# Feed-forward weights by float32 load and on-chip cast, RMS gain folded in, and a new order of all steps (linear attention, then SwiGLU)

## The chip, the cores and the metric

The kernel runs on one core of one Trainium2 chip. The metric is the device time of one execution in microseconds; the time before is the median of three runs. The profile is one further execution, recorded instruction by instruction. Engine names are those of the profile: PE (TensorE matmuls), PEld (its weight loads), DVE (VectorE), ACT (ScalarE), POOL (GpSimd), SP (SyncE, which issues most DMAs here).

## The reference

Two layers, one after the other, all in float32 at the boundary. B = 4 sequences, H = 8 heads, S = 768 steps, D = 48 per head; so 3072 tokens of H·D = 384.

```python
# linear attention with a decaying state, per (batch, head):
for t in range(S):
    y[t]  = r[t] @ (state + (u * k[t]) v[t]^T)
    state = w[t][:, None] * state + k[t] v[t]^T
# feed-forward on x = y, tokens x 384
rms = sqrt(mean(x * x, axis=-1) + 1e-6)
xn  = x / rms * rms_g
out = (silu(xn @ w_gate) * (xn @ w_val)) @ w_out     # 384 -> 1536 -> 384
```

## The kernel before

The sequence is cut into six blocks n = 0..5 of 128 steps; j = 0..3 is the batch. One attention step works on (n, j): 128 steps, 8 heads. One feed-forward step works on a block n: all four batches, so 512 tokens, and one of 12 groups f of 128 hidden units.

Every piece of work is a named step `name.n.j` (or `name.n.f`), and the string `ORDER` lists all of them. The kernel issues them in that order, and each engine and each DMA queue does its own part of them strictly in that order; semaphores are set where data or a buffer is needed. So the order is written out by hand, and an engine that waits holds up all that stands behind it in its own queue.

The steps of attention for one (n, j): `load_r`, `load_k`, `load_v`, `load_w` (SP, 192 KB each; in blocks 0 and 1 one `load_w` of 384 KB serves both); `ln` (ACT, logarithm of the decay); `cs_mm` (PE, running sums by a mask matmul), `cs_add` (DVE); `exp_r`, `exp_k` (ACT); `r_mul`, `k_mul` (DVE; `k_mul` on POOL from block 1); `rk_pe` (PE transposes) with `rk_tr` (ACT copy) in blocks 0 and 1, `rk_tr` alone (a transposing DMA from SP) later; `q_mm` (PE), `q_mask_e`, `q_copy_o`, `q_mask_o` (masks); `st_mm`, `st_new` (state); `bonus_mul`, `bonus_v` (POOL), `bonus_sum` (DVE); `cast_v` (ACT in blocks 0 and 1, POOL later); `y_mm` (PE), `x_add` (DVE).

Between the layers: `x_sq` (ACT, sum of squares), `x_rstd` (ACT in block 0, two POOL instructions later), `xn_mul` (ACT). Then x has to be transposed: in blocks 0 to 3 by `xn_pe` (three PE transposes) and `xn_out` (DVE, which also multiplies by rms_g); in blocks 4 and 5 by `xn_tr` (a transposing DMA from SP) and `xn_gain` (POOL, the multiplication by rms_g).

The feed-forward steps for a block: `gate_mm`, `val_mm` (three matmuls of 128x512 each), `silu` (ACT), `h_mul` (DVE), `o_mm` (12 matmuls of 128x384), `o_out` (copy), `out_dma`. `gate_mm` alternates between two PSUM banks (ring a), `val_mm` between two others (ring b); the rest uses four (ring q). ACT uses two function tables, one for exp and ln, one for silu, and reloads at each change.

The weights come by DMAs of POOL's software queue that cast from float32 to bfloat16 on the way: `load_gv.g.h` brings gate (h = 0) and value weights (h = 1) in two groups (`GV = (0, 4, 12)`: hidden groups 0 to 3, then 4 to 11), `load_wo.g` the output weights in three groups. `warm` steps are matmuls of zeros that compute nothing; there are 48 of them, all before or just at the start of the feed-forward of block 0.

Of the kernel before, what the change touches and what calls it, by code (L numbers as in the profile page):

```python
# [30 lines left out]
rk_pe.0.1 warm.15.0 warm.14.0 load_k.0.3 bonus_mul.0.3 load_r.1.1 load_r.1.0 load_k.1.1 load_v.1.1 load_r.1.2 ln.0.3
load_k.1.3 warm.20.0 warm.37.0 warm.2.0 warm.22.0 warm.23.0 warm.5.0 warm.3.0 rk_pe.0.0 warm.24.0 load_gv.0.1
load_k.1.2 load_v.1.0 load_w.2.1 warm.25.0 load_v.1.2 load_w.2.0 load_v.1.3 load_r.2.1 load_r.2.0 load_w.2.2 warm.32.0
warm.27.0 st_mm.0.0 st_new.0.0 load_w.2.3 cs_mm.0.2 rk_tr.0.1 q_mm.0.1 warm.19.0 rk_tr.0.0 exp_r.0.2 cast_v.0.1
r_mul.0.2 warm.7.0 cs_mm.0.3 q_mask_e.0.1 q_mm.0.0 warm.6.0 warm.18.0 warm.11.0 warm.26.0 warm.1.0 warm.21.0 warm.36.0
exp_k.0.2 w_tot.0.2 k_mul.0.2 rk_pe.0.2 q_mask_e.0.0 bonus_sum.0.2 bonus_v.0.2 exp_r.0.3 w_tot.0.3 q_mask_o.0.0
r_mul.0.3 warm.39.0 y_mm.0.0 warm.9.0 cs_mm.1.0 cast_v.0.3 q_mask_o.0.1 x_add.0.0 load_k.2.1 load_gv.0.0 cast_v.0.2
exp_k.0.3 k_mul.0.3 rk_tr.0.2 q_mm.0.2 q_mask_o.0.2 q_mask_e.0.2 y_mm.0.1 x_add.0.1 exp_r.1.0 bonus_sum.0.3 r_mul.1.0
rk_pe.0.3 cs_mm.1.1 x_sq.0.0 warm.34.0 x_rstd.0.0 rk_tr.0.3 q_mm.0.3 q_mask_o.0.3 exp_r.1.1 exp_k.1.0 exp_k.1.1
warm.40.0 warm.35.0 x_sq.0.1 x_rstd.0.1 xn_mul.0.0 xn_mul.0.1 y_mm.0.2 q_mask_e.0.3 warm.44.0 warm.42.0 x_add.0.2  # L40
warm.41.0 st_mm.0.3 st_new.0.3 warm.43.0 x_sq.0.2 x_rstd.0.2 w_tot.1.1 w_tot.1.0 bonus_v.0.3 y_mm.0.3 x_add.0.3
x_sq.0.3 xn_mul.0.2 x_rstd.0.3 xn_pe.0.0 xn_out.0.0 st_mm.0.2 xn_pe.0.1 cs_mm.1.3 exp_r.1.3 st_new.0.2 xn_out.0.1
r_mul.1.1 load_gv.1.0 k_mul.1.0 st_mm.0.1 warm.47.0 rk_pe.1.0 warm.45.0 st_new.0.1 xn_pe.0.2 xn_out.0.2 cs_mm.1.2
xn_mul.0.3 exp_k.1.3 xn_pe.0.3 r_mul.1.3 xn_out.0.3 cast_v.1.1 k_mul.1.1 load_gv.1.1 rk_pe.1.1 st_mm.1.1 exp_k.1.2
exp_r.1.2 w_tot.1.2 r_mul.1.2 w_tot.1.3 bonus_mul.1.3 val_mm.0.2 val_mm.0.3 warm.46.0 gate_mm.0.2 gate_mm.0.3 rk_tr.1.1
# [637 lines left out]
```

## Time and profile before

| | |
|---|---|
| median of the runs | 203.19 us (203.01, 203.19, 203.19) |
| span of the profiled execution, first to last instruction | 202.2 us |
| busy: PE, DVE, ACT, POOL | 192.6, 146.1, 136.6, 134.3 us |
| granted TensorE clock, mean | 0.999 |
| DMA moved | 32.41 MB, of it 28.58 MB on the hardware queue and 3.54 MB on the software queue |

The profiled execution is told by its span alone; the timed runs are 0.8 to 1.0 us longer than that span, and 1.0 us is taken here for what lies around it (203.19 less 202.2). In the lists below the two numbers in front of a row are the start and the duration in microseconds. "busy" of PE contains the modelled end of each matmul, so what a matmul costs is read from the distance between the starts of two that follow each other.

### The profile page before, as it was taken

To read this page: it belongs to the slowest core of one execution; us is meant where nothing else is said; L and a number is where in the kernel's file an instruction comes from. 1 tells how busy PE (TensorE), PEld (TensorE's weight loads), DVE (VectorE), ACT (ScalarE), POOL (GpSimd) and SP (SyncE) were. 2 spreads that over 40 slices of the span, in tenths; PEclk is the share of its full clock that TensorE was granted. 3 is DMA by queue.
4 is the path that set the end of the run, shared out by engine and by line. 5 is a ranking of instruction groups with operands and counts; after the bars stand their busy time and mean duration, and the time that the engine had idled before them with its cause. 6 is when DMAs were issued, how large, how long until landed. Compare 5 with 4: busy or idle time off the path is not lost.

```text
span 202.2 us, 4444 instructions
## 1 busy us (share of the span) xinstructions
PE 192.6 (95%) x1600; PEld 113.5 (56%) x1600; DVE 146.1 (72%) x289; ACT 136.6 (68%) x278; POOL 134.3 (66%) x198
## 2 busy tenths in 40 slices
PE   1999988899999999999999999999999999999994
PEld 1564655455666555665556665555555555555562
DVE  6257796658999699987988889788878972146521
ACT  2577699688998557997566978679867764046300
POOL 6527599658789966899789898859898742400000
PEclk9999999999999999999999999999999999999999
DMA  6999999989999999958999978996184022103022
GB/s 152 243 244 177 209 182 202 202 161 201 199 192 221 196 179 238 225 133 194 177 231 245 206 171 195 216 241 134 24 192 112 15 68 71 45 3 117 0 97 99
DMA packets 121566, 32.41 MB, mean 160 GB/s; under 512 B 116420, under 2 KB 120392, under 8 KB 121544
## 3 DMA queue, kind: packets, MB, share of 16 engines
q1 hardware_dynamic: 119504, 28.58, 67.2%
q0 software_dynamic: 2032, 3.54, 9.7%
q8 instruction: 12, 0.20, 0.4%
q14 instruction: 10, 0.08, 0.1%
q10 hardware_dynamic: 8, 0.00, 0.0%
HBM read 25.96 MB, written 4.72 MB: 152 GB/s over the span
## 4 chain that ended last, share of the span: by engine, by line
PE 79%; SPq 8%; DMA 8%; POOL 2%; issue 1%; ACT 0%; POOLq 0%
PE ps_av L598 12%; PE ps_bu L598 12%; PE ps_bv L598 10%; PE ps_au L598 10%; PE ps_qx L630 8%; PE ps_qv L630 7%; SPq L244 7%; DMA wg_sb<-in_moe_w_gate_dram 6%; PE ps_qz L630 5%; PE ps_qu L630 3%; SPq L257 2%; DMA kt<-in_k_dram 2%; PE ps_qu L487 1%; PE ps_av L406 1%; PE ps_qu L515 1%
## 5 line engine op out<-in xcount | busy, mean ns | idle before, releaser
L630 PEld LDWEIGHTS <-ht 128*128 128x128 bf16 x300 | 28.3, 98 | 16.9
L231 ACT ACTIVATE sg<-ps_av 128x512 bf16<-128x512 f32 x38 | 22.7, 598 | 18.4 <-PE ps_av L598 16.8
L616 DVE TENSOR_TENSOR ht<-ps_bu,sg 128x512 bf16<-128x512 f32 x38 | 26.1, 686 | 11.7 <-PE ps_bu L598 8.4
L598 PEld LDWEIGHTS <-wg_sb 128*128 128x128 bf16 x216 | 22.8, 114 | 20.2 <-DMA wg_sb<-in_moe_w_gate_dram 2.1
L598 PEld LDWEIGHTS <-wv_sb 128*128 128x128 bf16 x216 | 23.2, 114 | 19.3 <-DVE xnt L580 0.2
L616 DVE TENSOR_TENSOR ht<-ps_bv,sg 128x512 bf16<-128x512 f32 x34 | 23.3, 686 | 12.2 <-PE ps_bv L598 8.8
L452 POOL TENSOR_TENSOR ruk<-rt,kt 128x384 f32<-128x384 f32 x24 | 24.0, 1000 | 11.1 <-DMA kt<-in_k_dram 6.0
L598 PE MATMUL ps_av<-xnt,wg_sb 128*128 128x512 bf16 x114 | 30.9, 380 | 0.4 <-DMA wg_sb<-in_moe_w_gate_dram 0.4
L231 ACT ACTIVATE sg<-ps_au 128x512 bf16<-128x512 f32 x34 | 20.4, 599 | 16.0 <-PE ps_au L598 14.6
L598 PE MATMUL ps_bu<-xnt,wv_sb 128*128 128x512 bf16 x114 | 30.9, 380 | 0.0
L598 PE MATMUL ps_au<-xnt,wg_sb 128*128 128x512 bf16 x102 | 27.7, 381 | 0.8 <-DMA wg_sb<-in_moe_w_gate_dram 0.8
L598 PE MATMUL ps_bv<-xnt,wv_sb 128*128 128x512 bf16 x102 | 27.7, 380 | 0.0
L453 POOL TENSOR_TENSOR ruk<-ruk,u_bc 128x384 f32<-128x384 f32 x24 | 23.9, 997 | 1.9
L462 POOL TENSOR_TENSOR ydiag<-vt,diag 128x384 f32<-128x384 f32 x24 | 19.7, 830 | 0.9 <-DVE diag L457 0.8
L446 POOL TENSOR_TENSOR rk<-kt,ek 128x384 bf16<-128x384 f32 x20 | 19.9, 1003 | 0.3 <-ACT ek L231 0.3
L505 POOL TENSOR_SCALAR_AFFINE_SELECT qts<-qts 128x512 bf16<-128x512 bf16 x20 | 12.5, 636 | 10.7 <-ACT qts L498 10.7
L630 PE MATMUL ps_qx<-wo_sb,ht 128*128 128x384 bf16 x96 | 16.9, 326 | 0.0
L630 PE MATMUL ps_qv<-wo_sb,ht 128*128 128x384 bf16 (+1 forms) x96 | 15.9, 316 | 0.0
L558 ACT ACTIVATE xn<-xb,rstd 128x384 bf16<-128x384 f32 x24 | 14.1, 608 | 1.2 <-POOL rstd L554 1.2
L457 DVE TENSOR_REDUCE diag<-ruk 128x8 f32<-128x384 f32 x24 | 12.9, 543 | 2.7 <-POOL ruk L453 2.7
L231 ACT ACTIVATE lw<-wt 128x384 bf16<-128x384 f32 (+1 forms) x20 | 11.2, 579 | 4.6 <-DMA wt<-in_w_dram 4.5
L229 ACT ACT_TABLE_LOAD x10 | 12.8, 1283 | 1.8 <-PEq L667 1.6
(153 smaller groups left out, 368.2 us busy)
## 6 DMA issues: line engine op xcount, KB each, us to landing
rt<-in_r_dram SPq DMA_DIRECT2D x24, 192.0 KB, 3.9
kt<-in_k_dram SPq DMA_DIRECT2D x24, 192.0 KB, 3.9
vt<-in_v_dram SPq DMA_DIRECT2D x24, 192.0 KB, 3.7
out_dram<-ob SPq DMA_DIRECT2D x23, 192.0 KB, 2.1
wt<-in_w_dram SPq DMA_DIRECT2D x16, 192.0 KB, 3.9
wt<-in_w_dram SPq DMA_DIRECT2D x4, 384.0 KB, 4.6
wo_sb<-in_moe_w_out_dram POOLq DMA_DIRECT2D x3, 384.0 KB, 5.2
wg_sb<-in_moe_w_gate_dram POOLq DMA_DIRECT2D x1, 768.0 KB, 12.0
```

What stands on the lines that cost most here:

```text
L229: nc.scalar.preload_act_table_set(table_name)
L231: return nc.scalar.activation(**kw).ins
L244: dmas["load_" + which, n, j] = nc.sync.dma_start(out=inp[which, n, j], in_=t[j, :, n * L:(n + 1) * L, :].rearrange("h t d -> t h d")).ins
L446: eng.tensor_tensor(out=rk[:, n % 2, j, 1, :, 0:D], in0=inp["k", n, j], in1=bank["cs_k", n, j][:, 0:DM].rearrange("p (h d) -> p h d", h=H) ...
L452: nc.gpsimd.tensor_tensor(out=ruk[n, j], in0=inp["r", n, j], in1=inp["k", n, j], op=ALU.mult)
L453: nc.gpsimd.tensor_tensor(out=ruk[n, j], in0=ruk[n, j], in1=u_bc, op=ALU.mult)
L457: nc.vector.tensor_reduce(out=diag[n, j].rearrange("p h o -> p (h o)"), in_=ruk[n, j], axis=mybir.AxisListType.X, op=ALU.add)
L462: nc.gpsimd.tensor_tensor(out=ydiag[n, j], in0=inp["v", n, j], in1=diag[n, j].to_broadcast([128, H, D]), op=ALU.mult)
L558: nc.scalar.activation(out=xn, in_=xb[n, j], func=AF.Copy, scale=rstd[n, j][:, 1:2])
L598: nc.tensor.matmul(ps, lhsT=units(ws, c, f), rhs=xnt[n][:, c, :], start=(c == 0), stop=(c == KC - 1))
L616: nc.vector.tensor_tensor(out=ht[n][:, f, :], in0=bank.pop(("v", n, f)), in1=bank.pop(("sg", n, f)), op=ALU.mult)
L630: nc.tensor.matmul(ps[:, cols], lhsT=ht[n][:, f, b * L:(b + 1) * L], rhs=wo_sb[:, f, cols], start=(f == 0), stop=(f == FC - 1))
```

## The change

The weights are loaded as float32 by SP's hardware queue into staging buffers, nine loads of 768 KB: gate and value weights in three groups each (12 hidden units in groups of 4), output weights in three. There are four staging buffers: two of their own, and two that lie in one of the two buffers of `ht` (the hidden activations), which is free until block 1. New steps cast from there to bfloat16: `cast_gv.g.0` on ACT and `cast_gv.g.1` on DVE, three instructions of 128x512 each, multiplying by the column of rms_g that belongs to the partition; `cast_wo.g` on ACT, one instruction of 128x1536. With rms_g in the weights, `xn_out` becomes a plain copy and `xn_gain` is gone. `x_sq` scales by the root of 1/384 and has a 385th column that contributes eps, so `x_rstd` on POOL is one instruction instead of two. x lives in one buffer per batch (`xbuf`) instead of four rotating ones. Some rings are one smaller (`ydiag` 6 to 5, `rkT` 6 to 5, `ek` 4 to 3, `vb` 9 to 8).

The order of all steps is another one. In it blocks 2 and 3 transpose x by `xn_tr` too, so `xn_pe` and `xn_out` remain for blocks 0 and 1. There are 34 `warm` steps instead of 48, and some of them use the banks of rings a and b. ACT changes its function table four more times.

```diff
-    GV = (0, 4, 12)
     FG = 4
...
+    stage_own = persist.tile([128, 2, FG * DM], FP32)
+    stage_ht = pt.tile([128, 2, FG * DM], FP32, name="ht", bufs=NHT)
+    def stage(i):
+        return (stage_own, stage_own, stage_ht, stage_ht)[i % 4][:, i % 2]
     def load_gv(g, h):
...
-        i = nc.gpsimd.dma_start(out=dst[g], in_=s[:, cols].rearrange("(c p) f -> p c f", p=128)).ins
...
+        nc.sync.dma_start(out=stage(2 * g + h).rearrange("p (c f) -> p c f", c=KC),
+                          in_=(moe_w_gate, moe_w_val)[h][:, g * FG * 128:(g + 1) * FG * 128].rearrange(
+                              "(c p) f -> p c f", p=128))
+    def cast_gv(g, h):
+        s = stage(2 * g + h).rearrange("p (c f) -> p c f", c=KC)
+        for c in range(KC):
+            if (g, h) in GAIN_ACT:                      # gate weights
+                nc.scalar.activation(out=(wg_sb, wv_sb)[h][g][:, c, :], in_=s[:, c, :], func=AF.Copy, scale=gT[:, c:c + 1])
+            else:
+                nc.vector.tensor_scalar(out=(wg_sb, wv_sb)[h][g][:, c, :], in0=s[:, c, :], scalar1=gT[:, c:c + 1],
+                                        scalar2=None, op0=ALU.mult)
     def load_wo(g, _):
-        i = nc.gpsimd.dma_start(out=wo_sb[...], in_=moe_w_out[...]).ins
+        nc.sync.dma_start(out=stage(6 + g).rearrange("p (c m) -> p c m", c=FG), in_=moe_w_out[...])
+    def cast_wo(g, _):
+        dst, s = wo_sb[:, g * FG:(g + 1) * FG, :].rearrange("p c m -> p (c m)"), stage(6 + g)
+        nc.scalar.copy(out=dst, in_=s)                  # g in WO_ACT = (0, 1, 2)
...
     def x_sq(n, j):
-        nc.scalar.activation(out=junk, in_=xb[n, j], func=AF.Square, accum_out=rstd[n, j][:, 0:1])
+        nc.scalar.activation(out=junk, in_=xbuf[:, j], func=AF.Square, scale=DM ** -0.5,
+                             accum_out=rstd[n, j][:, 0:1])
...
     def x_rstd(n, j):                                   # blocks 1 to 5
-            nc.gpsimd.tensor_scalar(out=ss, in0=ss, scalar1=1.0 / DM, scalar2=eps, op0=ALU.mult, op1=ALU.add)
             nc.gpsimd.tensor_tensor(out=rstd[n, j][:, 1:2], in0=ss, in1=mhalf, op=ALU.pow)
...
     def xn_out(n, j):
-            nc.vector.tensor_tensor(out=xnt[n][:, :, j * L:(j + 1) * L], in0=ps,
-                                    in1=gT.to_broadcast([128, KC, L]), op=ALU.mult)
-    def xn_gain(n, c):
...
+        nc.vector.tensor_copy(out=xnt[n][:, :, j * L:(j + 1) * L], in_=ps)
```

The new order from the first weight load to the first output matmul of block 0, cut to the steps that the prediction speaks of (the rest of the list is as long again for each block):

```
... load_v.0.2 ... load_k.1.0 ... load_r.1.2 load_r.1.0 load_gv.0.0 ... load_gv.0.1 ... load_k.1.2 ... load_gv.1.0
... load_k.1.3 ... load_v.1.1 ... load_gv.1.1 ... xn_out.0.1 xn_mul.0.2 k_mul.1.2 cast_gv.0.0 xn_pe.0.2 ...
xn_out.0.2 cast_gv.0.1 gate_mm.0.3 exp_k.1.3 ... gate_mm.0.2 val_mm.0.2 ... silu.0.3 ... load_gv.2.0 ...
cast_gv.1.0 ... gate_mm.0.4 ... cast_gv.1.1 ... cast_gv.2.0 ... load_gv.2.1 ... load_wo.1.0 ... gate_mm.0.9 ...
load_wo.0.0 ... cast_gv.2.1 ... load_wo.2.0 ... cast_wo.1.0 ... cast_wo.0.0 ... cast_wo.2.0 ... o_mm.0.0 o_mm.0.2
```

More of the change, by code (lines that the diff above doesn't have):

```diff
@@ L31 @@
[L31 to L45, printed above, removed]
@@ new lines @@
+x_add.0.3 x_sq.0.3 q_mask_e.0.2 st_mm.0.3 warm.20.0 r_mul.1.3 ln.2.0 q_mask_o.0.2 bonus_v.0.2 cast_v.0.2 x_rstd.0.3
+w_tot.1.3 load_gv.1.0 st_new.0.0 rk_pe.1.1 warm.21.1 rk_tr.1.1 load_k.1.3 xn_mul.0.3 y_mm.0.2 warm.22.0 warm.23.1
+warm.24.1 warm.25.2 bonus_mul.1.1 x_add.0.2 q_mm.1.1 k_mul.1.0 x_sq.0.2 st_new.0.3 bonus_mul.1.0 st_mm.0.2
+q_copy_o.1.1 r_mul.1.0 w_tot.1.0 xn_pe.0.0 load_v.1.1 xn_out.0.0 cs_mm.1.2 x_rstd.0.2 xn_pe.0.3 bonus_sum.1.1
+q_mask_o.1.1 exp_r.1.2 xn_out.0.3 load_gv.1.1 rk_pe.1.0 exp_k.1.2 xn_pe.0.1 warm.26.1 warm.27.1 r_mul.1.2 w_tot.1.2
@@ L351, in load_wo @@
[L351 to L360 removed]
+    wg_sb = [persist.tile([128, KC, FG * 128], BF16, name="wg_sb%d" % g) for g in range(FC // FG)]
```

257 lines of the change are left out of this document (120 added, 137 removed).

## The prediction

> **What bounds the kernel now.** I read the busy shares by slice first, then the chain that ended last in order of time. On the page, one digit is the busy share of a fortieth of the span:
>
> ```profile
> span 202.2 us, 4444 instructions
> PE   1999988899999999999999999999999999999994
> ```
>
> The chain (start, duration, what):
>
> ```profile
> 18.64 3.76 DMA kt<-in_k_dram
> 22.47 1.00 POOL ruk L452
> ...
> 27.90 11.95 DMA wg_sb<-in_moe_w_gate_dram
> 39.90 0.84 PE ps_av L598 x3
> 40.74 0.65 PE ps_au L598 x3
> ...
> 198.30 1.00 PE ps_qu L630 x12
> 199.32 0.32 ACT ob L639
> ```
>
> Two parts. Up to 39.90 the chain is input loads on SP, then POOL, which issues a weight load late because it stands behind POOL's arithmetic, then that load. From 39.90 to 199.3 it is PE alone, one matmul behind another, three matmuls of 128x512 in 0.65 us. There no other engine's speed matters. So the change is worth three things: how much useful PE work is done by what time in the head, PE work taken away, and new gaps.
>
> **The head, by PE work.** Costs of steps are distances between starts, from the timeline of PE:
>
> ```profile
> 28.08 0.36 PE L535 MATMUL ps_qu<-vb,qts 128*128 128x48 bf16 x8
> 28.28 0.34 PE L569 MATMUL ps_qv<-ident,xn 128*128 128x128 bf16 x3
> 28.73 0.33 PE L515 MATMUL ps_qx<-vb,rk 128*128 128x96 bf16 x4
> 28.89 0.33 PE L569 MATMUL ps_qz<-ident,xn 128*128 128x128 bf16 x3
> 29.06 0.49 PE L391 MATMUL ps_av<-lw,mw 128*128 128x384 bf16 x2
> ```
>
> The first of these is a y_mm of block 0, 0.20 (28.08 to 28.28), the third a st_mm, 0.16, the fourth an xn_pe, 0.17. Both orders have the whole PE part of block 0 and the same steps of block 1 done when the dense part begins (eight cs_mm, six rk_pe, five q_mm, four y_mm, four xn_pe), with two differences: before 39.90 the old kernel has also done seven gate and value steps (7 x 0.65 = 4.55) and one st_mm (0.16), 4.7 us together. So a new dense part that starts with its first gate step at X corresponds to X + 4.7 against 39.90.
>
> X needs two things: the first gate weights cast, and x of block 0 through ACT (in the new order cast_gv.0.0 stands right behind xn_mul.0.2).
>
> *Transfers.* SP's issues:
>
> ```profile
> 0.80 0.45 SPq L244 DMA_DIRECT2D rt<-in_r_dram  x1
> ...
> 25.64 1.30 SPq L244 DMA_DIRECT2D vt<-in_v_dram  x1
> ```
>
> Between the two lie 25 issues, four of 384 KB and 21 of 192 KB: 5568 KB in 24.84 us, 224 KB per us. In the new order four of 384 and 19 of 192 stand ahead of load_gv.0.0: 5184 KB, so it is issued at 0.8 + 23.1 = 23.9. A weight chunk's own time comes from the two large loads, issue rows and times to landing:
>
> ```profile
> 27.90 0.80 POOL L346 DMA_DIRECT2D wg_sb<-in_moe_w_gate_dram  x1
> 30.63 0.80 POOL L346 DMA_DIRECT2D wv_sb<-in_moe_w_val_dram  x1
> kt<-in_k_dram SPq DMA_DIRECT2D x24, 192.0 KB, 3.9
> wg_sb<-in_moe_w_gate_dram POOLq DMA_DIRECT2D x1, 768.0 KB, 12.0
> wv_sb<-in_moe_w_val_dram POOLq DMA_DIRECT2D x1, 768.0 KB, 13.5
> ```
>
> They land at 39.9 and 44.1: 4.2 us for what is two new chunks (768 KB in bfloat16, 1536 KB read), so 2.1 each; at SP's 224 KB per us it would be 3.4, the other end. With 2.1, load_gv.0.0 lands at 23.9 + 3.9 + (2.1 - 0.9) = 29.0, load_gv.0.1 at 31.1, the other chunks with the inputs between them at 34, 38, 40, 44.7, 46.8, 48.9 and 51.0.
>
> *ACT.* From its first logarithm at 5.09 to its first silu table load at 34.65:
>
> ```profile
> 5.09:34.65 29.56, 28.23 (x298) 16.81 (x296) 20.08 (x46) 22.68 (x50) 19.39 (x22) 1.00 1.07 210
> ACT lw L231 <- DMA wt<-in_w_dram: 4.5, 2, 2.3
> ```
>
> The fourth pair of the first row is ACT: 22.68 busy, 6.9 idle. The new list up to cast_gv.0.0 has the same steps but for one exp_k and one cast_v less and one ln and one q_copy_o more: 22.8. Of the idle time 4.5 was two waits for load_w; the new order issues two of these first of all, so I take these waits as gone and keep 2.4 (ends: 0 and 6.9). The first load_w is issued one issue earlier, so ACT starts at 4.6: 4.6 + 22.8 + 2.4 = 29.8, after the landing at 29.0. Then the cast:
>
> ```profile
> L231 ACT ACTIVATE sg<-ps_av 128x512 bf16<-128x512 f32 x38 | 22.7, 598 | 18.4 <-PE ps_av L598 16.8 <-DVE ht L616 1.0
> L558 ACT ACTIVATE xn<-xb,rstd 128x384 bf16<-128x384 f32 x24 | 14.1, 608 | 1.2 <-POOL rstd L554 1.2
> L374 ACT CAST vb<-vt 128x384 bf16<-128x384 f32 x8 | 4.0, 504 | 0.7 <-DMA vt<-in_v_dram 0.7
> 32.05 0.47 ACT L231 ACTIVATE ek<-ps_bu 128x384 f32<-128x384 f32 x1
> 32.42 0.50 ACT L374 CAST vb<-vt 128x384 bf16<-128x384 f32 x1
> ```
>
> 128 more elements cost 0.094 us (598 against 504), a scale by partition 0.104 (608 against 504), and the next one starts 0.1 before the last ends (32.05 + 0.47 against 32.42). So one instruction of cast_gv is 0.504 + 0.094 + 0.104 - 0.1 = 0.60, a cast_gv 1.8. X = 31.6; 31.6 + 4.7 = 36.3; the dense part comes 3.6 earlier.
>
> **PE work taken away.** Blocks 2 and 3 lose eight xn_pe of 0.17: 1.35 us off the dense part.
>
> **New gaps.** First, o_mm.0.0 needs cast_wo.2.0 for its ninth matmul. From cast_gv.0.0 to the end of cast_wo.2.0 ACT has: three cast_gv 5.4; three cast_wo of 1536 elements, 0.504 + 9 x 0.094 - 0.1 = 1.25 each, 3.75; twelve silu 6.0; one table load; three rk_tr, three q_copy_o, four cast_v, two x_sq, an xn_mul and an exp:
>
> ```profile
> L229 ACT ACT_TABLE_LOAD x10 | 12.8, 1283 | 1.8 <-PEq L667 1.6
> L478 ACT COPY rkT<-ps_qz 128x1024 bf16<-128x1024 bf16 x3 | 3.0, 1007 | 1.4 <-PE ps_qz L469 1.4
> L498 ACT CAST qts<-ps_qv 128x512 bf16<-128x512 f32 x5 | 2.9, 581 | 1.1 <-PE ps_qv L489 1.1
> ```
>
> 1.3 + 3 x 0.9 + 3 x 0.48 + 4 x 0.4 + 2 x 0.6 + 0.5 + 0.4 = 9.1; together 24.3. So 29.8 + 24.3 = 54.1 without an idle moment, while PE, with 24 gate and value steps (15.6) and fourteen short attention steps (4.2, by such distances) between X and o_mm.0.0 and eight matmuls of 0.16 in it, is there at 31.6 + 21.1 = 52.7: a gap of 1.4. The last chunk (51.0) is not what is late. The Trainium skill, ScalarE: Activation LUTs, section What ACT_TABLE_LOAD costs, gives an instruction 186 ns and 0.833 ns per element: that agrees with 504 for 384, and would make a cast_wo 0.12 dearer and the total 0.35 us later.
>
> Second, the transposes of block 2. Behind y_mm.2.2 ACT has a table load, eight further steps of 0.4 to 0.6 and waits for POOL, xn_mul.2.2 ends about 6.1 behind it; the transposing DMA lands 2.7 later and SP's issue may stand behind another of 1.2:
>
> ```profile
> xnt<-xn SPq DMA_TRANSPOSE x8, 2.7
> 138.56 8.14 SPq L563 DMA_TRANSPOSE xnt<-xn  x3
> ```
>
> 8.9 to 10 against a cover of y_mm, two cs_mm, st_mm and four o_mm of 1.95: 8.9. I take 0.4, with ends 0 and 1.1. The last row is what this risks: three transposes held SP for 8.14 us, and all loads behind them. Blocks 3 to 5 have more cover than chain by the same count.
>
> At nothing: xn_gain, the shorter x_rstd and the weight issues leave POOL (about 15 us), which after 28 us is on no chain; the value casts on DVE (at most 0.6 an instruction, 1.8 each) replace eight xn_out. If that cover went, val_mm.0.2 would wait up to 0.5. The smaller rings and the single xbuf are freed a block earlier than they are needed. The table's four more loads (5.2 us of ACT) fall where ACT has more room: 17.11 busy of 20.67 between 34.65 and 55.32 is its tightest stretch before, and cast steps take that.
>
> Sum: 202.2 - 3.6 - 1.35 + 1.4 + 0.4 = 199.05 of span. The runs' median is 203.19, 1.0 over the span; with it 200.1.
>
> **Rivals.** (a) ACT's queue sets the head, with as much idle time as now, 6.9 instead of 2.4: everything 4.5 later, 204.6, slower. It decides from 5.9 on (203.6 is the bound below). For it: ACT's list has no spare step, and r, k and v come in another order too; against: 4.5 of the 6.9 has a named cause.
>
> (b) No gain from the queue. The Trainium skill, DMA: Bandwidth & Descriptors, section Issuing engines are not separate DMA queues, says that DMAs of all issuers share the same 16 engines and another issuer saves only issue time. Here, while the weights of the software queue were in flight, a load_w took up to 17.6 us to land instead of 3.9 (the instructions of its line):
>
> ```profile
> DMA to landing us min/median/max: 3.1/3.9/17.6
> ```
>
> So the trace agrees that they share. If the head is as long as its transfers, and those are not fewer, X + 4.7 stays 39.9: 203.19 - 1.35 + 0.4 = 202.2. Against it: by bytes, the first weights stand behind no more than before.
>
> (c) ACT waits for nothing: X is set by the landing at 29.0 (0.8 earlier), no gap at o_mm.0.0, none at the transposes: 200.1 - 0.8 - 1.4 - 0.4 = 197.5.
>
> **Chances.** Forecast 0.45 (its own range 198.8 to 201.5), (a) 0.22, (b) 0.13, (c) 0.20. Range: from just below (c), 197.3, to just above (a), 204.8, for weight chunks nearer 3.4. What a measurement of this kernel can tell from no change is 0.2%, 202.8 to 203.6. Faster: 0.44 + 0.20 + 0.05 = 0.69; same: 0.08, mostly the upper half of (b) with a later transpose; slower 0.23.
>
> **What would show it.** Right: first gate matmul of block 0 near 31.6, not behind a weight DMA but behind ACT's cast; o_mm.0.0 with a gap of 1 to 2 us named after ACT; ACT busy over 9 of 10 from 20 to 55; from then PE without gaps. Wrong: PE waiting for weight DMAs, ACT idle over 6 us before the first silu, or PE gaps at xnt in blocks 2 to 5.

## The result, and the profile of the changed kernel

| | before | changed |
|---|---|---|
| median of the runs | 203.10 us (202.75 to 203.19) | 210.12 us (209.34 to 211.15) |
| ratio, 95% interval | | 1.0352 [1.0313, 1.0392] |
| span of the profiled execution | 202.2 us | 207.7 us (its own time 209.39) |

The changed kernel is 3.5% slower; the forecast was 200.1, faster. In the times below, executions more than 1.5% above the fastest of the same kernel are left out: 214.64 of e2_loads_behind, 212.35 and 212.60 of e4_warm (its trace is of the 212.60) and 218.36 of e6_software_queue. The page of the changed kernel, the rows that answer to those shown of before, with the granted clock of PE by slice:

```profile
span 207.7 us, 4398 instructions
PE   1999797998899999994999996999999999999994
PEclk9999999999999999998899999999999999999999
```

Before, PE was at 9 in every slice from the ninth on (40 us), the last apart. Here there are a 4 in slice 19 and a 6 in slice 25, two 8s between 46 and 57 us, and two slices (19 and 20) in which the granted clock is below full. The timeline of PE (start, duration, line, what; in brackets the idle time ahead of it and who is named for it) at the three places where most is lost:

```profile
31.59 0.41 PE L588 MATMUL ps_av<-xnt,wg_sb 128*128 128x512 bf16 x1
32.20 0.41 PE L588 MATMUL ps_av<-xnt,wg_sb 128*128 128x512 bf16 x1 [0.21 <-ACT wg_sb L349]
...
35.00 0.41 PE L588 MATMUL ps_bv<-xnt,wv_sb 128*128 128x512 bf16 x1 [0.70 <-DVE wv_sb L351]
...
92.86 0.33 PE L522 MATMUL ps_qx<-vb,rk 128*128 128x96 bf16 x4
96.07 0.81 PE L588 MATMUL ps_bv<-xnt,wv_sb 128*128 128x512 bf16 x3 [2.88 <-DVE diag L464]
96.72 1.27 PE L588 MATMUL ps_au<-xnt,wg_sb 128*128 128x512 bf16 x3
97.79 1.49 PE L588 MATMUL ps_av<-xnt,wg_sb 128*128 128x512 bf16 x3
...
125.68 0.33 PE L522 MATMUL ps_qx<-vb,rk 128*128 128x96 bf16 x4
127.66 0.81 PE L588 MATMUL ps_bu<-xnt,wv_sb 128*128 128x512 bf16 x3 [1.64 <-issue]
```

The first row is gate_mm.0.3, the first step of the dense part, at 31.59. The rows at 96.07 and 127.66 are the first feed-forward steps of blocks 2 and 3. How the two kernels stand against each other by stage (starts of these steps on PE; for block 0 of the kernel before, 39.90 less the 4.7 us of work that it had done by then):

| | before | changed | difference |
|---|---|---|---|
| feed-forward of block 0 | 35.2 | 31.59 | -3.6 |
| feed-forward of block 1 | 64.49 | 65.07 | +0.6 |
| first output matmul of block 1 | 84.25 | 84.53 | +0.3 |
| feed-forward of block 2 | 93.24 | 96.07 | +2.8 |
| first output matmul of block 2 | 112.13 | 116.93 | +4.8 |
| feed-forward of block 3 | 121.86 | 127.66 | +5.8 |
| feed-forward of block 4 | 149.54 | 155.02 | +5.5 |
| end of the span | 202.2 | 207.7 | +5.5 |

Everything is decided by 128 us. I took each distance between the starts of two following matmuls, and the usual one of its kind (its median in the profile); the sum of what exceeds it is lost time. From its first gate step the changed kernel loses 12.0 us so, the one before 1.4 us from 39.90. Of the 12.0: block 0's feed-forward 4.5; ahead of block 2's 3.05, and 1.7 in its first matmuls (eight of them start 0.43 apart instead of 0.216; the expectations below count 1.87); ahead of block 3's 1.8; the rest, 0.9, is the small change that the kernel before has too. The sum of the usual distances is 160.9 us here and 157.55 there, which differ by 3.35, as 4.7 - 1.35 does. (How the kinds are cut moves the lost time of both kernels alike; their difference stays between 10.1 and 10.6.) So the span is 202.2 - 3.6 (start) - 1.35 (PE transposes gone) + 10.6 (waits) = 207.9, and it is 207.7. This is the account of the two profiled executions, 5.5 us apart; the medians are 7.0 apart.

### The profile page after: what moved, and what is told of

The parts are those of the page before. It is cut to its first block, busy times and chain, and to the rows that moved or that the text cites. A ratio compares the mean times of both kernels' runs of the same rounds, so it can differ in the third digit from the quotient of the medians.

```text
span 207.7 us, 4398 instructions
## 1 busy us (share of the span) xinstructions
PE 192.2 (93%) x1562; PEld 112.0 (54%) x1562; DVE 147.4 (71%) x289; ACT 150.0 (72%) x294; POOL 119.9 (58%) x164
## 2 busy tenths in 40 slices
DMA packets 125694, 36.73 MB, mean 177 GB/s; under 512 B 119780, under 2 KB 122984, under 8 KB 125672
## 4 chain that ended last, share of the span: by engine, by line
PE 62%; ACT 13%; DMA 8%; DVE 6%; issue 5%; SPq 3%; POOL 1%; POOLq 0%; DVEq 0%
PE ps_av L588 9%; PE ps_bv L588 9%; PE ps_au L588 9%; PE ps_bu L588 9%; DMA stage_own<-in_moe_w_val_dram 7%; PE ps_qu L620 5%; PE ps_qx L620 4%; PE ps_qv L620 3%; PE ps_qz L620 3%; SPq L239 3%; DVE wv_sb L351 2%; ACT junk L551 2%; DMA out_dram<-ob 2%; ACT wo_sb L362 2%; ACT xn L564 2%
## 5 line engine op out<-in xcount | busy, mean ns | idle before, releaser
L606 DVE TENSOR_TENSOR ht<-ps_bv,sg 128x512 bf16<-128x512 f32 x38 | 26.0, 685 | 17.5 <-PE ps_bv L588 13.9
L231 ACT ACTIVATE sg<-ps_au 128x512 bf16<-128x512 f32 x36 | 21.7, 604 | 21.7 <-PE ps_au L588 19.5
L588 PE MATMUL ps_bv<-xnt,wv_sb 128*128 128x512 bf16 x114 | 31.1, 380 | 3.8 <-DVE diag L464 2.9
L588 PE MATMUL ps_bu<-xnt,wv_sb 128*128 128x512 bf16 x102 | 28.5, 387 | 2.1 <-issue 1.6
L588 PE MATMUL ps_au<-xnt,wg_sb 128*128 128x512 bf16 x108 | 29.7, 385 | 0.0
L606 DVE TENSOR_TENSOR ht<-ps_bu,sg 128x512 bf16<-128x512 f32 x34 | 23.3, 686 | 4.5 <-PE ps_bu L588 4.1
L560 POOL TENSOR_TENSOR rstd<-rstd,mhalf 128x1 f32<-128x1 f32 x20 | 11.1, 558 | 20.1 <-ACT junk L551 19.9
L564 ACT ACTIVATE xn<-xbuf,rstd 128x384 bf16<-128x384 f32 x24 | 14.6, 611 | 1.2 <-POOL rstd L560 0.6
L620 PE MATMUL ps_qu<-wo_sb,ht 128*128 128x384 bf16 x84 | 14.8, 326 | 0.0
L551 ACT ACTIVATE junk<-xbuf 128x385 bf16<-128x385 f32 x24 | 12.6, 526 | 2.0 <-DVE xbuf L546 1.9
```

The costliest lines, as they stand in the source:

```text
L231: return nc.scalar.activation(**kw).ins
L551: nc.scalar.activation(out=junk, in_=xbuf[:, j], func=AF.Square, scale=DM ** -0.5, accum_out=rstd[n, j][:, 0:1])
L564: nc.scalar.activation(out=xn, in_=xbuf[:, j, 0:DM], func=AF.Copy, scale=rstd[n, j][:, 1:2])
L588: nc.tensor.matmul(ps, lhsT=units(ws, c, f), rhs=xnt[n][:, c, :], start=(c == 0), stop=(c == KC - 1))
L606: nc.vector.tensor_tensor(out=ht[n][:, f, :], in0=bank.pop(("v", n, f)), in1=bank.pop(("sg", n, f)), op=ALU.mult)
L620: nc.tensor.matmul(ps[:, cols], lhsT=ht[n][:, f, b * L:(b + 1) * L], rhs=wo_sb[:, f, cols], start=(f == 0), stop=(f == FC - 1))
```

## The experiments

All were compared with the kernel before on the same chip, whose medians there were 202.8 to 203.1. Most of the later ones build on e1_pe_transpose, the changed kernel with PE transposes.

**Who holds up blocks 2 and 3.** The chain of waits of the changed kernel, up to the matmul at 96.07 (start, duration, what):

```profile
86.91 1.71 SPq L239
88.67 0.59 SPq L239
89.30 0.66 SPq L251
90.00 3.50 DMA out_dram<-ob
93.53 0.56 DVE ob L627
...
95.61 0.47 DVE diag L464
96.09 0.80 PE ps_bv L588 x3
```

Read as it stands, PE waits for DVE, which waits for an output buffer. The timeline of SP's queue tells another story (L569 is xn_tr):

```profile
84.24 2.62 SPq L569 DMA_TRANSPOSE xnt<-xn  x2
86.91 1.71 SPq L239 DMA_DIRECT2D vt<-in_v_dram  x1
88.67 0.59 SPq L239 DMA_DIRECT2D kt<-in_k_dram  x1
89.30 0.66 SPq L251 DMA_DIRECT2D wt<-in_w_dram  x1
90.00 1.25 SPq L635 DMA_DIRECT2D out_dram<-ob  x1
91.35 1.20 SPq L569 DMA_TRANSPOSE xnt<-xn  x1
92.59 0.58 SPq L251 DMA_DIRECT2D wt<-in_w_dram  x1
93.27 1.20 SPq L569 DMA_TRANSPOSE xnt<-xn  x1
```

The last transpose is issued at 93.27 and its own landing is 2.7 us later, 95.98; ACT had its input ready at 89.83 (xn_mul.2.2, 89.22 and 0.61 long). Three experiments tell the two apart.

```diff
 # e1_pe_transpose: blocks 2 and 3
-xn_tr.2.0 xn_tr.2.1 xn_tr.2.3 xn_tr.2.2   (and xn_tr.3.*)
+xn_pe.2.0 xn_out.2.0 ...                  (xn_pe.2.2, 3.1 and 3.2 between output matmuls)
```

> Blocks 2 and 3 transpose x on PE again (xn_pe and xn_out in place of xn_tr); all else is the changed kernel, whose profiled execution took 209.4. Theory Q, the queue: the gaps of 3.05 us ahead of block 2's feed-forward (st_mm.2.3 at 92.98, val_mm.2.5 at 96.07) and of 1.81 ahead of block 3's are there because the transposing DMAs stand in SP's queue behind loads and an output DMA (xn_mul.2.2 ends at 89.83, its transpose is issued at 93.27). Then both gaps go, and with the first of them the 1.87 us by which the matmuls after it are slow: 209.4 - 3.05 - 1.81 - 1.87 + 8 x 0.17 = 204.0. Theory O, the output buffers: DVE stands at o_out.1.0 from 90.81 to 93.53 because the buffer is held by out_dma.0.1, and what DVE does late behind it holds up PE; then a gap of at least 1 us stays and the time is 206 or more. Theory X, x itself is late through ACT and POOL: the gaps stay, 210.7.

Measured: 206.19 (205.26 to 207.69), ratio 1.0166 [1.0111, 1.0221]. Both gaps are gone and PE's granted clock is 0.998:

```profile
93.43 0.33 PE L523 MATMUL ps_qv<-vb,rk 128*128 128x96 bf16 x4
93.60 0.81 PE L589 MATMUL ps_bv<-xnt,wv_sb 128*128 128x512 bf16 x3
```

The profile's own time is 205.26 against 209.39, 4.1 less where theory Q had 5.4: its block 0 started 0.6 later (first gate step at 32.22), and a gap of 0.73 appeared ahead of block 4, behind the transposing DMAs that are left. The median, 206.19, is the number of theory O, but the gap that theory O keeps is not there.

```diff
 # e2_loads_behind: SP's order only
-load_v.4.0 load_w.4.1 ... xn_tr.2.3 load_w.4.3 xn_tr.2.2
+xn_tr.2.3 xn_tr.2.2 load_w.4.1 load_v.4.0 load_w.4.3        (block 3: load_k.4.2 load_v.5.2 load_k.5.3 behind xn_tr.3.1)
```

> Only SP's order is changed: in block 2 load_w.4.1, load_v.4.0 and load_w.4.3 move behind xn_tr.2.2, in block 3 load_v.5.2, load_k.5.3 and load_k.4.2 behind xn_tr.3.1. Theory Q: xn_tr.2.2 is issued at about 90.0 and lands at 92.7, xn_tr.3.1 is issued at about 122.6 and lands at 125.5; both gaps go and so does the slow stretch: 209.4 - 6.7 = 202.7, or up to 204 if a moved load is then late. Theory O: out_dma.0.1 is issued some 2.4 us earlier too, so DVE is freed at about 91 and the first gap goes as well, but the one of block 3 (1.81) stays: 204.5. Theory X: 209.4.

Measured: 210.20 to 212.97, ratio 1.0414 [1.0348, 1.0480]. The timeline of SP:

```profile
89.17 2.50 SPq L569 DMA_TRANSPOSE xnt<-xn  x2
```

and of PE:

```profile
92.94 0.81 PE L588 MATMUL ps_bv<-xnt,wv_sb 128*128 128x512 bf16 x3
...
95.51 0.81 PE L588 MATMUL ps_bu<-xnt,wv_sb 128*128 128x512 bf16 x3 [0.47 <-ACT ek L231]
97.42 0.81 PE L588 MATMUL ps_au<-xnt,wg_sb 128*128 128x512 bf16 x3 [1.10 <-ACT sg L231]
...
132.34 0.81 PE L588 MATMUL ps_bu<-xnt,wv_sb 128*128 128x512 bf16 x3 [3.21 <-DVE ht L606]
```

Theory Q is right on the place: with the two transposes ahead of the loads, block 2's feed-forward starts at 92.94, 3.1 earlier and without a gap. It is wrong on the price: what was moved back comes late in its turn. ACT waits 2.7 us for a load_w, q_mm of block 3 for its transposes (1.3), and in block 3 DVE waits 5.4 us for an output buffer, whose output DMA now stands behind the moved loads. SP's queue had no slack to give here.

```diff
 # e3_out_early
-... out_dma.0.0 (block 3)
+o_out.0.0 out_dma.0.0
```

> out_dma.0.0 moves from block 3 to right behind o_out.0.0, so that one of the three output buffers is no longer held for 80 us. Theory O: DVE no longer stands at o_out.1.0 (2.7 us) and the gap ahead of block 2's feed-forward goes with the slow stretch: 209.4 - 3.05 - 1.87 = 204.5. Theory Q: DVE's wait goes, but xn_tr.2.2 is still issued at about 93.3 and PE starts block 2 at about 96.1 as before: 209.4, within 0.7. Theory X: 209.4.

Measured: 211.71 (210.56 to 212.71), ratio 1.0412 [1.0372, 1.0451]. DVE's wait for the output buffer ahead of block 2 is gone, the gap is not, and now it is named after what it waits for (the last transpose is issued at 94.65):

```profile
97.73 0.81 PE L588 MATMUL ps_bv<-xnt,wv_sb 128*128 128x512 bf16 x3 [3.24 <-DMA xnt<-xn]
```

So theory O falls as the cause ahead of block 2, and with it the chain's reading: where two waits end within 0.1 us of each other, the chain names the one that ended last, and the other stands ready behind it. The time itself is 1.6 us above the changed kernel's, outside theory Q's 209.4 within 0.7. In the trace o_mm.0.0 already starts 1.1 us later (55.99) and the gap ahead of block 3 has grown to 2.7 us; why the early output DMA does that is open.

**The slow matmuls.**

```diff
 # e4_warm
+warm.34.2 ... warm.49.2   (ahead of val_mm.2.5)
```

> Sixteen matmuls of zeros (0.163 us each, 2.6 us) are put between st_mm.2.3 and val_mm.2.5, where PE stands idle for 3.05 us in the changed kernel. They compute nothing. Theory C, the clock: the matmuls from 96.1 to 100 start 0.42 to 0.43 us apart instead of 0.216 because PE's clock falls after an idle stretch of 3 us; then the start of block 2's feed-forward stays at 96.1, its length falls from 20.86 to 19.0 us and the time by 1.87: 207.5. Rival: these matmuls are slow because of something else that is going on at that time (operands, other engines' traffic); then the feed-forward still takes 20.9 and the time stays 209.4.

Measured: 209.19 and 210.73, ratio 1.0344 [1.0293, 1.0396]. The zeros were dearer than thought: 6.0 us instead of 2.6, because each waits for the bank of the one before it (0.38 from start to start), so block 2 starts at 99.9 and the saving is eaten. Its feed-forward then took 19.2 us instead of 20.9, with the matmuls 0.216 apart from the first on. One execution is little to go by; the windows of two others say more (stretch, its length, busy time and instructions of PE, PEld, DVE, ACT, POOL, then PE's granted clock, DMA share, GB/s). The changed kernel:

```profile
94.00:96.00 2.00, 0.00 (x0) 0.00 (x0) 2.00 (x8) 1.24 (x1) 1.92 (x3) 1.00 0.89 201
96.00:98.00 2.00, 1.93 (x7) 0.94 (x8) 1.11 (x3) 0.00 (x0) 0.26 (x1) 0.73 0.95 199
98.00:100.00 2.00, 2.00 (x6) 0.69 (x5) 0.69 (x1) 1.56 (x3) 1.84 (x3) 0.50 1.17 270
```

and e3_out_early:

```profile
98.00:100.00 2.00, 2.00 (x11) 1.08 (x10) 0.14 (x1) 0.77 (x2) 0.64 (x1) 1.00 1.18 221
130.00:132.00 2.00, 2.00 (x7) 0.80 (x6) 1.11 (x2) 0.60 (x1) 2.00 (x3) 0.55 1.01 235
132.00:134.00 2.00, 2.00 (x7) 0.71 (x6) 1.63 (x4) 0.62 (x2) 1.03 (x2) 0.60 1.08 212
```

In the changed kernel the clock falls behind the gap of 3.05 us, and the matmuls start 0.42 us apart instead of 0.216. In e3_out_early it stayed full behind 3.4 us without work (94.3 to 97.7) and fell behind 2.9 us (126.2 to 129.1). The Trainium skill, TensorE: Matmul & The Clock Gate, section What's actually happening, has an idle window of about 3.4 us that is not tied to the work, half clock behind it, and a varying moment. The half clock and the variation agree with these rows; that a gap has to be 3.4 us long does not, since 2.9 and 3.05 were enough.

The traces show more of what decides. In every one that has a clock record the granted clock changes only at whole multiples of 3.41 us from its first entry, so one can lay windows on that grid and ask how long PE was idle in each. In the changed kernel PE was idle for 2.56 us of the window from 93.52 to 96.93, and the clock was half in the next one, to 100.34. In e3_out_early the gap of 3.4 us was split by the edge at 96.06 into 1.57 and 1.67 us, and the clock stayed full; the shorter gap had 2.31 us in the window from 126.79 to 130.20, and the next window was at half clock. Over all these traces, full-clock windows with 2.05 us or more of idle PE were followed by half clock, those with 1.63 or less were not; between the two it went either way (1.67 in e6_software_queue: half; 1.70 in e2_loads_behind: full). So it is not the length of a gap alone that decides but also where it falls on the grid, and the program does not set that: the record's first entry lies 9.0 to 12.1 us into the span. Here the half clock cost 1.7 us on top of the gap.

Of the four runs of the changed kernel one had a mean clock of 0.999 where the profiled one had 0.992, and took 209.34 us, no less; so the clock by itself does not make the slow result.

**Block 0: the landing, the casts, or the engines.** The chain of the changed kernel, cut to the two weight loads and what hangs on them:

```profile
25.18 7.70 DMA stage_own<-in_moe_w_val_dram
32.90 2.06 DVE wv_sb L351 x3
...
41.33 6.12 DMA stage_own<-in_moe_w_val_dram
47.48 0.04 DVE wv_sb L351
...
53.50 1.36 ACT wo_sb L362
...
55.37 1.36 ACT wo_sb L362
```

```diff
 # e5_gv21_early (on e1_pe_transpose)
-load_gv.2.0 ... load_v.1.3 ... load_v.1.0 ... load_v.1.2 load_gv.2.1
+load_gv.2.0 load_gv.2.1 ... load_v.1.3 ... load_v.1.0 ... load_v.1.2
 # e7_w20_late (on e1_pe_transpose): load_w.2.0 behind load_wo.0.0, ln.2.0 ahead of ln.2.1, cs_mm.2.0 behind o_mm.0.0
 # e8_wo2_pool (on e1_pe_transpose)
-    WO_ACT = (0, 1, 2,)
+    WO_ACT = (0, 1)
```

> On the kernel with PE transposes in blocks 2 and 3 (206.2), load_gv.2.1 moves on SP from behind load_v.1.3, load_v.1.0 and load_v.1.2 to right behind load_gv.2.0, so that it is issued at about 35.6 instead of 41.2. Theory L, the landing: cast_gv.2.1 on DVE starts at 47.2 only because its load lands at 47.17; val_mm.0.9 waits for it (1.05 us), and because DVE stands, silu.0.10 and the three cast_wo behind it on ACT come late, which makes the gaps of 0.41 and 0.58 at o_mm.0.0. Then all three go: 206.2 - 2.0 = 204.2. Theory A, ACT is full: the gap at val_mm.0.9 goes, those at o_mm.0.0 grow by as much: 206. Theory D, the DMA engines are full there: what is moved back (load_v.1.0, load_v.1.2) is late in its turn and PE waits for y_mm of block 1: 206.2 or more.

Measured: 205.38 (205.06 to 205.70), ratio 1.0119 [1.0068, 1.0170]. The gap of 1.05 at val_mm.0.9 is gone and so is that of 0.41 ahead of o_mm.0.0, which starts at 53.67 instead of 54.62; the one inside it (0.58, behind the third cast_wo) stays. Between theories L and A: the gap at val_mm.0.9 went with the late landing, the one inside o_mm.0.0 did not. (That of 0.41 is back in e11_two_mended, where the load is early too, so its cause is open.) Ahead of block 4 the gap grew to 1.45. The interval of the time overlaps that of e1_pe_transpose; it is the trace that shows the gain, block 1's feed-forward starting at 63.83 instead of 64.78.

> On the kernel with PE transposes in blocks 2 and 3 (206.2), cast_wo.2.0 goes from ACT to POOL, which is idle from 50 to 55. Theory A, ACT is what o_mm.0.0 waits for: the 0.58 us inside o_mm.0.0 go, and ACT has 1.4 us more for what follows: 205.6, or 205.2 if ACT's later steps were late too. Theory L: the load of these weights lands at 52.9 and POOL's cast takes 4 x 0.5 = 2 us, so it ends at 54.9 or a little later, and nothing is gained beyond 0.58: 205.6. If POOL's cast is slower than 3.5 us, o_mm.0.0 waits longer than before and the time is 206.5 or more.

Measured: 205.32 (205.09 to 205.61), ratio 1.0117 [1.0066, 1.0167]. POOL's cast took what ACT's does, 1.46 us, and the 0.58 are gone; from o_mm.0.0 to block 1's feed-forward it is 9.26 us instead of 10.16 (here too the interval of the time overlaps that of e1_pe_transpose):

```profile
53.32 1.46 POOL L365 CAST wo_sb<-stage_own 128x1536 bf16<-128x1536 f32 x1 [3.65 <-DMA stage_own<-in_moe_w_out_dram]
```

> On the kernel with PE transposes in blocks 2 and 3 (206.2), load_w.2.0 leaves SP's queue ahead of the first weights and goes behind load_wo.0.0; ln.2.0 and cs_mm.2.0 go to the place of ln.2.1 and behind o_mm.0.0. Theory L, the landing of the first weights sets the start: they are issued 0.8 us earlier, gate and value weights land 0.8 us earlier, the first gate step and the gap at val_mm.0.2 with them: 205.4. Theory A, ACT sets it (29.7 at best, 0.4 less without ln.2.0): the first gate step comes at most 0.4 earlier, 205.8. Theory D, the DMA engines are full and the landing depends on the bytes of all that is in flight, not on the place: 206.2.

Measured: 207.64 (206.87 to 207.97), ratio 1.0236 [1.0176, 1.0295]. The first weights were issued at 22.94 instead of 24.18, and the first gate step came at 30.87, 1.3 earlier than in e1_pe_transpose. That is little proof that the start hangs on what stands ahead of the weights in SP's queue, since runs that leave the head as it is start anywhere from 31.04 (e11_two_mended) to 32.56 (e5_gv21_early). And ln.2.0 behind the change of tables made cs_mm.2.0 late (1.2 us), and block 1's feed-forward started at 66.04, 1.3 later. The step that I moved away was where it cost least.

**The two halves of the change.**

```diff
 # e6_software_queue (on e1_pe_transpose): load_gv and load_wo on nc.gpsimd, straight into wg_sb, wv_sb, wo_sb; no cast steps
 # e12_old_order: the changed functions with the ORDER of before; load and cast steps put in by hand
```

> The order of the kernel with PE transposes in blocks 2 and 3 (206.2), but the weights come as in the kernel before: nine casting DMAs of POOL's software queue, at the same places of the list, straight into bfloat16, and no cast steps. rms_g is multiplied in xn_out in blocks 0 to 3; blocks 4 and 5 leave that multiplication out. So only the way of the weights is put back. Theory W, the hardware queue is what brings the first weights early: here they land about 12 us after their issue at 24, the first gate step comes at 36 or later instead of 32.2, the gaps of 3.6 us behind casts go: 206.2 + 3.8 - 3.6 = 206.4, or later. Theory S, all transfers share the DMA engines and the queue brings nothing: the weights land at 31 to 33 all the same, no casts stand on ACT and DVE (9.65 and 6.1 us), and the gaps go: 202.6. Theory R, the new order alone is the loss: about 206 with the gaps of block 0 still there.

Measured: 213.86 to 216.80, ratio 1.0625 [1.0533, 1.0717]. The first gate step comes at 40.3, in the range of theory W, but the weights did not arrive late (7.1 us from issue to landing for the first). What was late is the input that shared the DMA engines with them:

```profile
DVE rk L425 <- DMA rt<-in_r_dram: 6.4, 1, 6.4
```

A load_r of block 1, issued at 22.67, landed at 34.28, 11.6 us later; in the changed kernel the same load was issued at 22.61 and landed at 26.34. The next one, load_r.1.0, issued at 23.57, was there at 34.88; r_mul.1.0 waited for it on DVE, and x of block 0 (xn_out) stood behind r_mul.1.0. PE stood 5.95 us behind that, and its clock was half from 31.78 to 42.02. Both queues use the same DMA engines, as the Trainium skill says (DMA: Bandwidth & Descriptors, section Issuing engines are not separate DMA queues), and the run agrees. The next sentence of the Trainium skill there says that starting DMAs on several engines saves only issue time. Here the kernel with the second queue was 10 us slower, and the measurement decides: a second queue can also cost. In SP's queue the loads landed in the order of their issue; here a weight load issued at 26.11 landed at 34.18, ahead of the load_r issued at 22.67, so the order in which data is needed is lost. What share of the 10 us this has is not shown, since the casts, the half clock and POOL as the issuer changed with it.

> The other half of the change by itself: the order of the kernel before, with the weights by float32 loads on SP, staging and casts. load_gv.0.0 and 0.1 stand on SP where load_gv.0.1 stood on POOL, load_gv.1.0 and 1.1 behind load_v.1.3, the others behind the casts that free their buffers; each cast stands ahead of the first step that needs it. Theory N, the new order is the loss and the way of the weights by itself is none: block 0's feed-forward no longer waits for weights on POOL's queue (5 us between its first and its eighth step), so 203.1 or up to 3 less. Theory P, the loads take SP's queue and DMA engines from block 2's loads and the casts take ACT and DVE: gaps in the feed-forward of blocks 0 and 1 of 3 us or more, 205 or later.

Measured: 221.58 (220.99 to 222.32), ratio 1.0922 [1.0864, 1.0980]. Theory P, but far beyond its size: PE was busy 14.5 of 20 us between 40 and 60, and from 60 to 80 the DMA engines were 0.34 busy, because SP's queue stood: it issued nothing from 57.1 to 75.2. The granted clock was 0.83 and 0.91 in these two stretches. The places of the loads and casts are mine, so this holds for one careless order, not for every one; it shows that the new way of the weights can cost some 19 us in an order that was not made for it.

**Putting the mends together.**

```diff
 # e11_two_mended = e1_pe_transpose + e5_gv21_early + e8_wo2_pool
 # e9_three_mended = e11_two_mended, and block 4:
-xn_tr.4.1 xn_tr.4.3 xn_tr.4.2
+xn_pe.4.1 xn_out.4.1 o_mm.3.2 ... xn_pe.4.3 xn_out.4.3 xn_pe.4.2 xn_out.4.2 o_mm.3.1
 # e10_split_cast = e9_three_mended, and in cast_gv:
+            if (g, h, c) == (0, 1, 1):
+                nc.gpsimd.tensor_scalar(...)        # middle third of the first value group
 # and (0, 0, 1) on DVE; cast_gv.0.0 behind xn_out.0.2, k_mul.1.2 behind cast_gv.0.1
 # e13_casts = e11_two_mended + the split casts, cast_wo.0.0 ahead of cast_wo.1.0
 # e14_two_back = e13_casts with xn_tr.2.0 and xn_tr.3.0
```

> Together: PE transposes in blocks 2 and 3 (206.2 alone), load_gv.2.1 early (0.8 less), cast_wo.2.0 on POOL (0.9 less), and PE transposes for three of the four batches of block 4 as well, placed between the output matmuls, where a gap of 1.1 to 1.45 us ahead of block 4's feed-forward had appeared behind the transposing DMAs (three transposes cost PE 0.5). If the waits are independent: 206.2 - 0.8 - 0.9 - 0.7 = 203.8. If they share a cause (the DMA engines, which are full until 130 us), what is gained in one place is lost in the next: 205.

Measured: 210.58 (209.94 to 211.19), ratio 1.0375 [1.0342, 1.0407]: a miss. Between the output matmuls the PE transposes wait for DVE (PE's timeline):

```profile
149.90 2.12 PE L621 MATMUL ps_qz<-wo_sb,ht 128*128 128x384 bf16 x12 [0.91 <-DVE st L530]
...
152.67 0.33 PE L576 MATMUL ps_qz<-ident,xn 128*128 128x128 bf16 x3 [0.48 <-DVE ob L628]
153.87 2.11 PE L621 MATMUL ps_qv<-wo_sb,ht 128*128 128x384 bf16 x12 [0.86 <-DVE xnt L582]
```

All four banks of ring q are taken there, since o_out.3.3 and st_new.4.2 come late in the list; each new tenant waits for a DVE step that stands in a full queue. I had counted PE's work and ACT's times, not the banks. These rows account for some 3 us: from o_mm.3.0 to block 4's feed-forward it is 11.4 us, and 8.4 in e11_two_mended below. Another 3.8 us were lost before (block 3's feed-forward starts at 125.20 instead of 121.37), although the steps are the same up to there; the loads fell behind from 25 us on, the last weights landing at 55.13 instead of 53.13. Why is open.

> As the kernel with three waits mended, and the casts of the first gate and value weights are split: the middle third of the gate group goes from ACT to DVE, the middle third of the value group from DVE to POOL (k_mul.1.2 stands behind it there). If PE waits there for the casts: the first gate step is complete 0.7 us earlier and val_mm.0.2 another 0.65: 203.8 - 1.3 = 202.5. If it waits for the landings (30.3 and 32.4 to 32.9), the start is where it was and only what the cast takes behind the landing is saved, about half: 203.2. If POOL's or DVE's new work holds up what stands behind it (k_mul.1.2, st_new.0.2): 204 or more.

Measured: 210.21 (209.66 to 210.57), ratio 1.0357 [1.0323, 1.0392]; 0.4 less than the kernel that it builds on, with intervals that overlap. In its trace val_mm.0.2 stands 0.93 us for POOL's third of the cast, so it is the third case that came.

> PE transposes in blocks 2 and 3, load_gv.2.1 early and cast_wo.2.0 on POOL, without the PE transposes of block 4, which cost 3.8 us of new gaps around the output matmuls of block 3. If the two mends of block 0 add up: 206.2 - 0.8 - 0.9 = 204.5. If they share a cause, the DMA engines that are full until 130 us, block 1's feed-forward starts no earlier than with one of them, or is held up inside, as it was with three mends: 205.4 or more.

Measured: 204.24 (203.41 to 205.94, 10 runs), ratio 1.0088 [1.0059, 1.0118]. The time fits the case that the two mends of block 0 add up (204.5), but its interval touches that of e1_pe_transpose; the trace is clearer: block 1's feed-forward starts at 62.74, where e1_pe_transpose has 64.78 and the two mends by themselves 63.83 and 64.21. It is the fastest kernel of the new order, and not faster than the one before. Its profiled execution (span 201.7, the shortest of its runs) has the same account: first gate step at 31.04, 4.2 us ahead of before in the same count as above; 5.0 us lost in waits against 1.4; PE's work as before. 202.2 - 4.2 + 3.6 = 201.6.

> On the kernel with PE transposes in blocks 2 and 3, load_gv.2.1 early and cast_wo.2.0 on POOL (204.2): the casts of the first gate and value weights are split (the middle third of the gate group to DVE, of the value group to POOL), and cast_wo.0.0 goes ahead of cast_wo.1.0 on ACT. If PE waits there for the casts themselves: 0.41 at o_mm.0.0 go, 0.4 of the first gate step's 0.8 and the 0.53 behind val_mm.0.2: 204.2 - 1.3 = 202.9, level with the kernel before. If it waits for the landings (31 and 33), only the 0.41 and a part of the rest go: 203.6. If the new order has no more room on DVE and POOL: 204.2 or more.

Measured: 205.67 (205.50 to 205.76), ratio 1.0143 [1.0124, 1.0162]: slower than without the split. POOL is not as fast at this cast as at the plain one:

```profile
L350 POOL TENSOR_SCALAR wv_sb<-stage_own,gT 128x512 bf16<-128x512 f32 x1 | 1.9, 1862 | 2.2 <-DMA stage_own<-in_moe_w_val_dram 2.2
L355 DVE TENSOR_SCALAR wg_sb<-stage_own,gT 128x512 bf16<-128x512 f32 x1 | 0.5, 485 | 0.1
```

With 1.86 us for a third it held val_mm.0.2 for 1.2 us, and what followed came late. The gap ahead of o_mm.0.0 went with the new order of the two cast_wo, but one of 0.66 opened inside it, for the other of the two.

> As the kernel with the split casts, but the first batch of blocks 2 and 3 goes back to transposing DMAs (xn_tr.2.0, xn_tr.3.0), which have 8 us to spare before PE needs them. PE loses 0.34 us of work. If only the place in SP's queue counts, a transpose that is early enough costs nothing: 0.34 less than the kernel with the split casts, 202.6. If SP's queue has no room in those stretches at all (each transpose holds SP for 1.2 to 1.3 us and all loads behind it), loads of block 3 and 4 come late and the time is 0.5 us or more above that kernel: 203.4 or more.

Measured: 206.09 (205.42 to 206.77), ratio 1.0165 [1.0139, 1.0191]; 0.4 above e13_casts, with intervals that overlap, so the direction is likely and the size open. PE has 0.34 us less to do, and up to block 3's feed-forward that is gained (122.81 instead of 123.21). It is lost ahead of block 4's, where PE stands 1.34 us instead of 0.63 and the wait is named after a transposing DMA: an early transpose is free on its own path, but it holds SP for 1.2 us and moves back what stands behind it. That this is what made block 4's transpose late fits the trace and was not tested by itself.

## Why the prediction was wrong, step by step

**The start X: right, by two errors that cancel, and by luck to the hundredth.** 31.6 was forecast, 31.59 measured; later runs with the same head started from 31.04 to 32.56. ACT was through with xn_mul.0.2 at 29.7 (29.8 forecast). But load_gv.0.0 landed at 30.79, not 29.0, and ACT stood 1.09 us for it; and PE started behind the first third of the cast, not behind all of it. So the first gate step is on time and its three matmuls are 0.61 apart:

```profile
30.82 1.95 ACT L349 ACTIVATE wg_sb<-stage_own,gT 128x512 bf16<-128x512 f32 x3 [1.09 <-DMA stage_own<-in_moe_w_gate_dram]
```

A cast_gv took 1.95 instead of 1.8, on DVE 2.06. The cast of the value weights, which I had at nothing or 0.5, cost 0.86: its load landed at 32.9 instead of 31.1, and the last of its three instructions took 1.25 us (33.70 to 34.95) where the first two took 0.49 and 0.48. "At most 0.6 an instruction" was mis-sized. In nine of the traces every such DVE cast with POOL idle took 0.47 to 0.49 us, and every one of more than 0.5 us ran while POOL worked (at 33.70 it was k_mul, from 33.67 to 34.66); not every overlap had this effect. The chunks followed each other by about 2 us as forecast, but those whose landing the trace tells came 1.3 to 2.8 us later than forecast.

**PE's work: right**, 1.35 less, by the sum of the usual distances.

**The gap at o_mm.0.0: nearly right in size, in cause only in part.** 1.4 was forecast, 0.41 + 0.58 came. The 0.58 is the wait for cast_wo.2.0 behind ACT's other work, as forecast: it stayed when the load came early (e5_gv21_early) and went when the cast left ACT (e8_wo2_pool). The cause of the 0.41 is open. And load_gv.2.1, forecast to land at 44.7, landed at 47.45: SP stood 3.8 us at the issue of load_v.1.2 ahead of it, where I had let SP issue at a steady 224 KB per us:

```profile
37.43 3.80 SPq L239 DMA_DIRECT2D vt<-in_v_dram  x1
41.33 0.66 SPq L341 DMA_DIRECT2D stage_own<-in_moe_w_val_dram  x1
```

With that landing came another gap, 0.97 at val_mm.0.9, which no part of the forecast has and which e5_gv21_early takes away. In all, block 0's feed-forward lost 4.5 us where the forecast has 1.4. A cast_wo took 1.465 us, 0.1 more than my working allowed. The Trainium skill, ScalarE: Activation LUTs, section What ACT_TABLE_LOAD costs, gives 186 + 0.833 x 1536 = 1466 ns for it, and the trace agrees.

**The transposes of block 2: the step that failed.** Forecast 0.4, with ends 0 and 1.1; measured 3.05, and 1.7 more through the clock. The chain of compute was right (xn_mul.2.2 ends 5.7 us behind the start of y_mm.2.2, 6.1 forecast), the landing was right (2.7), the cover was right (8.8 of 8.9). Wrong was one term: "SP's issue may stand behind another of 1.2". It stood 3.4 us behind four issues, another transpose and an output DMA among them. The row of three transposes that hold SP for 8.14 us was quoted as a risk and not priced. In these rows an issue on SP took 0.58 to 1.71 us, where the first load of the kernel before took 0.45. That the DMA engines were full, before as after (a share of 0.89 to 1.13 in every 20 us from 20 to 120), is the likely reason and was not tested. A window of the kernel before, the DMA share being the number ahead of the last:

```profile
80.00:100.00 20.00, 20.00 (x185) 12.27 (x182) 17.72 (x39) 16.20 (x34) 17.45 (x24) 1.00 0.97 191
```

and of the changed one:

```profile
100.00:120.00 20.00, 20.00 (x185) 11.72 (x184) 17.23 (x32) 13.69 (x29) 13.08 (x19) 0.99 1.07 212
```

**Blocks 3 to 5: also wrong.** "More cover than chain" by compute, and 1.8 us lost in block 3 by the same queue: the last transpose is issued at 124.35 and lands at 127.57, and PE starts at 127.66.

**The rivals.** (a) had the sign, by a mechanism that did not happen: up to xn_mul.0.2 ACT was idle for 3.0 us (2.4 forecast), not 6.9. (b) is refuted by the changed kernel itself, whose X + 4.7 is 36.3 and not 39.9; e6_software_queue, 10 us slower with the weights on the software queue, points the same way. (c) had its condition, an X set by a landing, but the landing was 30.79 instead of 29.0, and the gaps that it puts at nothing were the loss. The 1.0 us around the span was 1.7 in all later runs (202.47 against 200.8 for the kernel before in one of them), a further 0.7; by that, the profiled execution of the kernel before was one of about 203.9, above its median.

The sum, then: -3.6 and -1.35 came as forecast; the waits were forecast at 1.8 and came to 10.6. The step that failed is the term for SP's queue ahead of the transposes, 1.2 us where 3.4 were measured, with what hung on it in blocks 2 and 3 (6.5 us in all, the clock included, where 0.4 was forecast); the late chunks and slow casts of block 0 added 3.1.

## What to carry to other kernels

When a step moves from a compute engine to a DMA, price its place in the issuing queue, at the issue times of a full queue, and price what then stands behind it; here the landing alone (2.7 us) was the smaller part of the 6.1 from ready input to landing. Where the DMA engines are full, moving a load forward moves another back: look for the load that has nothing waiting for it, and there may be none. Read the chain of waits as one candidate; if a second wait ends at nearly the same time, take the first away and see whether the gap goes.

## What the runs showed of the hardware

- Gaps of 2.9 to 3.05 us on PE halved the granted clock for one window of 3.41 us; one of 3.4 us that an edge of the window grid split in 1.57 and 1.67 did not.
- SP's issue of one 192 KB load took up to 4.24 us in the changed kernel (a load_r at 48.67) and 6.49 us in the one before (a load_v at 30.66); the median of such issues between 20 and 120 us was 0.73 and 0.78.
- With the weights on a second queue, an input load took 11.6 us to land instead of 3.7, though fewer bytes were moved (32.41 MB against 36.73).
- POOL cast 128x1536 from float32 to bfloat16 in 1.46 us, as fast as ACT; a third of that with a scale by partition took it 1.86 us, where ACT took 0.70 to 0.80 and DVE 0.47 to 0.49 with POOL idle and up to 1.25 beside a working POOL.
